# When a router is prepared, which engine copies sums, one projection at full height: four edits to a planned linear attention and mixture-of-experts kernel

## The chip, the cores and the metric

The kernel runs on one core of one Trainium2 chip. The core has a matrix engine (TensorE, PE in the profile; its weight loads, PEld, overlap the matmuls), a vector engine (VectorE, DVE), a scalar engine with activation functions (ScalarE, ACT), a general one (GpSimd, POOL), and SyncE (SP), which here only issues DMA transfers. Each engine runs its own instructions strictly in order; semaphores hold an instruction back until what it needs is there. The metric is the device time of one execution in microseconds (us), as the median of several runs. Before the change it is 818.04 us (817.71 to 819.43 in 3 runs).

## The reference

Three stages follow each other on 2304 tokens (4 batches of 576) of width 512 (8 heads of 64). Cut to what is computed:

```python
def phi(x):                                   # features, 64 -> 128
    proj = einsum('bhsd,md->bhsm', x, omega)
    h = proj - sum(x * x) / 2
    return exp(h - max(h)) / sqrt(m)
q_p, k_p = phi(q * scale), phi(k * scale)
kv = einsum('bhsm,bhsd->bhmd', k_p, v)        # sums over a batch's tokens
z = sum(k_p, axis=2)
x = einsum('bhsm,bhmd->bhsd', q_p, kv) / (einsum('bhsm,bhm->bhs', q_p, z) + 1e-6)

xn = x / sqrt(mean(x * x) + 1e-6) * rms_g     # a gated MLP, 512 -> 1536 -> 512
g = xn @ w_gate
x = (g * sigmoid(g) * (xn @ w_val)) @ w_out

logits = x @ w_gate2 + modality_bias[modality_id]   # top-1 of 8 experts, 512 -> 1024 -> 512
e = argmax(logits)
out = max(softmax(logits)) * (relu(x @ w1[e]) @ w2[e])
```

All inputs are float32 but the modality (int64); the output is float32.

## The kernel before, in words

**Tiles.** The tokens are 18 tiles of 128 (tiles 0 to 17). The attention takes k tiles and q tiles by name: k0 to k17, q0 to q17. Each tile has 8 heads in two units g = 0 and 1 of four heads. The order of the first nine is written out: "k0 k1 k2 k3 k4 q0 q1 q2 q3"; the others are woven into the MLP behind.

**One tile of the attention.** Its load (L520) brings x transposed, two heads (2 x 64 rows) on the 128 partitions. A projection (`projections`) multiplies it by omega in 8 products of 128 columns. omega is held twice in one tile of 128 x 256, as a block-diagonal matrix (`omega2`: rows 0 to 63 hold it in columns 0 to 127, rows 64 to 127 in columns 128 to 255, the rest is zero). So a projection can run in two forms: at full height (128 rows, L564, where the other head's rows meet zeros), which before is used for k0 and k1 alone, or at half height (64 rows, L571), used for all others. The trace counts two records for each product, sixteen for a tile. Then VectorE takes a maximum per head (L588), ScalarE the exponentials (L594). A k tile then adds its products with v to the batch's sums (L643, one group of eight records for each unit), a q tile is transposed (L609), copied out of the bank (L321 by `copy_on`), multiplied with the sums (L795) and divided (L820 and on).

**Seeds.** A batch has 576 tokens, so every other boundary falls in the middle of a tile. For a k tile that straddles two batches, the second batch's share is summed in a bank of its own and copied to a tile `seed` (L766, on VectorE); it is added when the batch's sums are closed.

**The router's small inputs.** `fetch_small` loads the router's weights, the modalities and the two biases. `bias_of_tokens` (L473 to L484) makes a bias for each token on VectorE, `split_route` (L486 to L490) splits the weights into three bfloat16 parts in five VectorE instructions (L489 and the subtraction in the helper `rest`, L325). Their first reader is the routing of the first finished tile (product L1328, scores L1348 to L1353), far later. The gain vector `rms_g` is loaded by `fetch_g` (L1403) and scaled on VectorE (L1409 to L1421).

**The MLP and the experts.** The MLP runs over 9 chunks of 256 tokens: transposes of its input (L1170), hidden products (L1192) for 12 blocks of 128 features, output products (L1262). All weights come as float32 and are split into two float16 halves (scalings and remainders on VectorE, ScalarE and GpSimd; L325 is the remainder's line on every engine). The tokens are then dealt to slots of 128 rows, one expert each: a first table for the tokens of tiles 0 to 15 (six "early" slots) and a full table later, whose place numbers end in the products of L1913. Each slot gathers its rows from memory by an indirect DMA on GpSimd (`gather`), is transposed, multiplied by the expert's matrices (up L2136, down L2165) and scattered to the output (L2033).

**What sets the order: a planner.** The kernel doesn't issue instructions in the order of its loops. Each step is an operation `plan.op(engine, cost, want, function, ...)` with a cost in us, a due number `want` and the buffers it reads and writes. `Plan.schedule` (L172 and on) plays the program through: whenever an engine is free it takes, of the operations whose inputs are ready and whose buffers can be had, the one with the smallest `want`. Where an operation may run on several engines (a dict of costs, engine `None`), whichever is free first takes it, but VectorE, in the main part, only when it has nothing of its own to do (`key`). An operation's users become ready `lag` after its end. The result is one fixed order per engine. Before that, `NUDGES` shifts due numbers: (first, last, shift, kind) adds `shift` to the operations of these numbers, of one kind if one is given.

**Padding.** `spare` plans 140 matmuls (L505) that nobody reads, with a due number of 1e9: the planner puts one wherever TensorE would otherwise have nothing ready. They stand in the program and always run.

**Loads.** SyncE issues the loads in one queue, in planned order. Eight semaphores are dealt to the transfers in turn, so a load may wait for an earlier one, and for TensorE or others who still read its buffer.

## Time and profile before

| | us |
|---|---|
| median of 3 runs (lowest, highest) | 818.04 (817.71, 819.43) |
| the profiled execution | 813.95 |
| its span | 812.2 |
| busy: TensorE | 795.9 |
| busy: VectorE | 546.5 |
| busy: ScalarE | 467.7 |
| busy: GpSimd | 290.3 |

The profile records one execution. The span runs from its first to its last instruction; the time of the execution has a little more around it. A timeline lists an engine's instructions as runs of one line: where it starts, how long it takes, and in brackets how long the engine was idle before it and what ended that. On TensorE neighbouring records overlap in their modelled ends, so the price of a group is read from its start to the start of the next. The list of waits adds up an engine's idle time by the instruction that waited and the one it waited for. A line of the page is that of the instruction, which for helpers is the helper's.

### The profile page before, as it was taken

Reading aid. Unit: us, or ns where it says so; the run is one execution under the profiler, and the core shown is the slowest. Engines: PE = TensorE matmul, PEld = TensorE weight load, DVE = VectorE, ACT = ScalarE, POOL = GpSimd, SP = SyncE. Lnnn points to the kernel's source line nnn. Section 1 sums busy time; section 2 is a strip of 40 time slices with the busy share of each in tenths; the row PEclk is TensorE's granted clock in tenths of the full one; section 3 lists DMA queues with packets and bytes.
Section 4 is the critical chain, followed back from the end, with each engine's and each line's share of the span. In section 5 each row is a group of like instructions: output and inputs, shape, how many; then the busy total and the mean of one; then the engine's idle time right before and its main releaser. Section 6 shows DMA issues by size and latency. Waiting matters only on the chain.

```text
span 812.2 us, 20349 instructions
## 1 busy us (share of the span) xinstructions
PE 795.9 (98%) x8128; PEld 627.9 (77%) x8128; DVE 546.5 (67%) x1299; ACT 467.7 (58%) x1118; POOL 290.3 (36%) x424
## 2 busy tenths in 40 slices
PE   9999999999999999999999999999999999999995
PEld 8999888988566878887878877777776778777772
DVE  5778888998348788898998888778767212222121
ACT  5767667777444777777787878666242322323221
POOL 0267898673213233223333343323222211212011
PEclk9999999999999999999999999999999999999998
DMA  8526341347111764776777677864726989999950
GB/s 279 173 62 234 136 143 40 96 157 287 47 40 54 250 218 130 246 273 223 234 229 235 201 240 230 272 245 181 280 75 266 411 295 406 425 410 425 425 228 29
DMA packets 37253, 179.31 MB, mean 221 GB/s; under 512 B 4863, under 2 KB 4991, under 8 KB 21280
## 3 DMA queue, kind: packets, MB, share of 16 engines
q1 hardware_dynamic: 34144, 168.33, 58.0%
q0 software_dynamic: 3008, 9.61, 3.2%
q8 instruction: 66, 1.08, 0.5%
q14 instruction: 35, 0.29, 0.1%
HBM read 134.90 MB, written 43.16 MB: 219 GB/s over the span
## 4 chain that ended last, share of the span: by engine, by line
PE 79%; DVE 6%; issue 5%; POOL 4%; DMA 4%; ACT 1%; POOLq 0%; ACTq 0%
PE bank L1192 28%; PE bank L1262 17%; PE bank L2136 8%; PE bank L2165 7%; PE bank L643 4%; PE bank L571 4%; DMA out_dram<-plain,x 2%; PE bank L795 2%; PE bank L505 2%; PE bank L609 2%; POOL plain L1230 1%; POOL big L325 1%; PE bank L1301 1%; PE bank L1995 1%; PE bank L1170 1%
## 5 line engine op out<-in xcount | busy, mean ns | idle before, releaser
L1192 PE MATMUL bank<-x,big 128*128 128x256 f16 x2592 | 307.3, 273 | 0.1
L1192 PEld LDWEIGHTS <-big 128*128 128x128 f16 x2592 | 250.2, 98 | 43.0 <-issue 0.7
L1262 PE MATMUL bank<-big 128*128 128x512 f16 x648 | 157.2, 379 | 0.0
L325 POOL TENSOR_TENSOR big<-plain,big 128x256 f16<-128x256 f32 x97 | 80.0, 827 | 135.1 <-ACT big L315 98.3
L880 DVE SCALAR_TENSOR_TENSOR big<-big,e_fac 128x512 f16<-128x512 f32 x128 | 102.6, 805 | 8.0 <-ACT big L886 6.5
L1262 PEld LDWEIGHTS <-big 128*128 128x128 f16 x648 | 62.4, 99 | 53.1
L2136 PEld LDWEIGHTS <-big 128*128 128x128 f16 x1632 | 95.6, 98 | 8.5
L2136 PE MATMUL bank<-plain,big 128*128 128x128 f16 x1632 | 100.6, 219 | 0.0
L2165 PE MATMUL bank<-big,plain 128*128 128x512 f16 x408 | 96.7, 379 | 0.0
L1211 ACT ACTIVATE plain<-bank,w_scale 128x256 f32<-128x256 f32 x108 | 50.6, 472 | 57.4 <-PE bank L1192 44.6
L1101 ACT ACTIVATE plain<-big,plain 128x1024 bf16<-128x1024 f32 x64 | 73.4, 1147 | 12.5 <-DMA big<-in_w_exp_dram 11.3
L325 DVE TENSOR_TENSOR plain<-plain 128x512 f16<-128x512 f32 (+2 forms) x42 | 27.3, 652 | 67.6 <-ACT plain L315 55.5
L594 ACT ACTIVATE plain<-bank,plain 128x128 f32<-128x128 f32 x216 | 61.1, 383 | 12.3 <-DVE plain L588 12.1
L886 ACT ACTIVATE big<-big,e_fac 128x512 f16<-128x512 f32 x95 | 67.8, 719 | 0.6 <-DMA split_dram<-big 0.6
L2165 PEld LDWEIGHTS <-plain 128*128 128x128 f16 x408 | 37.5, 98 | 35.7
L1216 DVE SCALAR_TENSOR_TENSOR plain<-plain,bank 128x256 f32<-128x256 f32 x108 | 44.4, 415 | 18.9 <-ACT plain L1211 13.7
L588 DVE TENSOR_REDUCE plain<-bank 128x4 f32<-128x512 f32 x72 | 47.8, 683 | 9.1 <-PE bank L564 4.8
L2153 ACT ACTIVATE plain<-bank 128x512 f32<-128x512 f32 x34 | 20.4, 599 | 57.0 <-PE bank L2136 55.1
L315 ACT CAST big<-plain 128x256 f16<-128x256 f32 x84 | 33.8, 405 | 29.6 <-DVE plain L1238 16.8
L325 DVE TENSOR_TENSOR plain<-bank,plain 128x512 f32<-128x512 f32 (+2 forms) x38 | 25.2, 666 | 29.6 <-ACT plain L315 29.3
L1230 POOL TENSOR_TENSOR plain<-plain,big 128x256 f32<-128x256 f32 x35 | 36.0, 1035 | 10.7 <-DVE plain L1216 9.7
L325 POOL TENSOR_TENSOR plain<-plain 128x512 bf16<-128x512 f32 (+1 forms) x22 | 24.7, 1124 | 32.4 <-DVE plain L325 22.7
(302 smaller groups left out, 1161.5 us busy)
## 6 DMA issues: line engine op xcount, KB each, us to landing
big<-split_dram SPq DMA_DIRECT2D x60, 1024.0 KB, 13.2
big<-in_w_exp_dram SPq DMA_DIRECT2D x32, 1024.0 KB, 6.5
split_dram<-big SPq DMA_DIRECT2D x32, 1024.0 KB, 8.6
big<-in_w_moe_dram SPq DMA_DIRECT2D x36, 512.0 KB, 3.7
x_dram<-plain SPq DMA_DIRECT2D x18, 258.0 KB, 3.1
plain<-in_qT_dram SPq DMA_DIRECT2D x14, 256.0 KB, 3.8
plain<-in_v_dram SPq DMA_DIRECT2D x13, 260.0 KB, 3.4
plain<-in_kT_dram SPq DMA_DIRECT2D x13, 256.0 KB, 4.3
```

The lines of the kernel that those rows point to most:

```text
L325: eng.tensor_tensor(out=out, in0=src, in1=hi, op=ALU.subtract)
L588: lambda: nc.vector.tensor_reduce(out=mx.tile, in_=pp.tile, axis=AX.X, op=ALU.min),
L594: nc.scalar.activation(ph[:, h, :], pp[:, h, :], AF.Exp, bias=mx[:, h : h + 1], scale=-1.0)
L880: nc.vector.scalar_tensor_tensor(out=out, in0=src, scalar=factor, in1=hi, op0=ALU.mult, op1=ALU.subtract)
L886: nc.scalar.activation(out, src, AF.Copy, scale=factor)
L1101: lambda c=c, h=h, cs=cs: nc.scalar.activation(junk.tile, raws[c][:, cs], AF.Square, bias=tiny, accum_out=sums[:, 2 * c + h : 2 * c + h + ...
L1192: nc.tensor.matmul(gv[:, t, :], w[a][:, kk, :], self.x[x][:, kk, :], start=kk == 0 and m == 0, stop=kk == KD - 1 and m == 2,)
L1211: lambda: nc.scalar.activation(th.tile, gv[:, 0, :], AF.Tanh, scale=one(BACK)),
L1216: lambda: nc.vector.scalar_tensor_tensor(out=th.tile, in0=th.tile, scalar=1.0, in1=gv[:, 0, :], op0=ALU.add, op1=ALU.mult,),
L1262: nc.tensor.matmul(self.acc[j].tile, h[:, a, r], out_w[f][:, i, :], start=f == 0 and m == 0, stop=f == FT - 1 and m == 2,)
L2136: nc.tensor.matmul(ph[:, j, :], w_of(c, p, k * F2 + (4 * n + j) * P, P), x[a][:, kk, :], start=kk == 0 and j == 0 and m == 0, stop=kk == K ...
L2165: nc.tensor.matmul(y.tile, hs[n][a][:, kk, :], w_of(2 + n, p, kk * DM, DM), start=f == 0 and m == 0, stop=f == KF2 - 1 and m == 2,)
```

## The change

Six edits. `WHOLE` becomes a list of names, "k0 k1 q1": the projection of q1 is done at full height as well. The due numbers of `bias_of_tokens` and `split_route` go from -150 and -140 to 28 and 29. The copies of the seeds may run on ScalarE or VectorE. The planner's lag of an early gather goes from 3 to 7. A pair of buffers (`qkx`) that nobody uses is gone. And `NUDGES` has 41 entries in place of 34, most with other numbers. The lines behind the table stand one line later in the changed kernel: L564 is L565.

```diff
--- before.py
+++ after.py
@@ -40,7 +40,7 @@
 THIRD_FROM, THIRD = 21.0, 0.65
 LAST_FROM, LAST = 26.5, 0.3
 EXACT = 6
-WHOLE = 2
+WHOLE = "k0 k1 q1"
 SPARE = 140
 NEARLY = 6
 NFULL = 17
@@ -50,15 +50,16 @@
 
 
 NUDGES = (
-    (927, 2712, 6.75, 61), (245, 713, 6.5, 39), (708, 753, 12), (252, 358, -9), (0, 1691, 7, 7),
...
+    (927, 2712, 6.75, 61), (247, 713, 6.25, 39), (250, 357, -8.25), (0, 1691, 7.5, 7),
...
 )
 
 
@@ -363,7 +364,7 @@
     STAGE, EXPERT = 36 * KB, 32 * KB
     area(
         "big", ("rawy", 8192, 2), ("bitsy", 4096, 2),
-        ("qkx", 2048, 2), ("phx", 2048, 2), ("ftx", 2048, 1),
+        ("phx", 2048, 2), ("ftx", 2048, 1),
         ("mxx", 16, 2), ("mod_i", 144, 1), ("mod_f", 208, 1), ("part", 576, 1),
         ("w_r", 128, 1),
     )
@@ -492,8 +493,8 @@
 
     plan.op("dma", 0.3, -170, fetch_small, writes=[mod_i, mod_f, w_r])
     route_b = Buf()
-    plan.op("dve", 0.5, -140, split_route, writes=[w_r, route_b])
-    plan.op("dve", 1.5, -150, bias_of_tokens, reads=[mod_i], writes=[mod_f, part, small_b])
+    plan.op("dve", 0.5, 29, split_route, writes=[w_r, route_b])
+    plan.op("dve", 1.5, 28, bias_of_tokens, reads=[mod_i], writes=[mod_f, part, small_b])
 
 
     def spare(n, before):
@@ -555,7 +556,7 @@
                 buf(named("ph", "phx"), [P, 4, NF], F32),
             ))
 
-        whole = kind == "k" and i < WHOLE
+        whole = f"{kind}{i}" in WHOLE.split()
 
         def products():
             for j in range(NPAIR):
@@ -762,9 +763,9 @@
                 acc = buf("acc", [P, 4, D + 1], F32)
                 kv_add(b, straddle[gg], whole[1][0], gg, *whole[1][1:], True, True, want, acc)
                 plan.op(
-                    "dve", 0.35, want,
-                    lambda acc=acc, gg=gg: nc.vector.tensor_copy(
-                        seed[:, 4 * gg : 4 * gg + 4, :], acc.tile
+                    {"act": 0.33, "dve": 0.35}, None, want,
+                    lambda e, acc=acc, gg=gg: copy_on(
+                        e, seed[:, 4 * gg : 4 * gg + 4, :], acc.tile
                     ),
                     reads=[acc], fills=[seed],
                 )
@@ -2009,7 +2010,7 @@
                     in_offset=bass.IndirectOffsetOnAxis(ap=ix[:rows, 0, col : col + 1], axis=0),
                 ),
                 reads=[ix, *(x2_b[:TE] if early else x2_b)], writes=[xg],
-                lag=3.0 if early else 8.0,
+                lag=7.0 if early else 8.0,
             )
             return xg
 
```

SyncE's queue of the start, before the change, with what each transfer waits for (big is the area that holds the tiles loaded first, DMAHW an earlier transfer's semaphore, PE the progress of TensorE):

```order
L528 DMA big_103<-in_v_dram 128x520 [waits DMAHW2_49]
L520 DMA big_103<-in_kT_dram 128x512 [waits DMAHW4_49,DMAHW3_49,PE_49]
L520 DMA big_103<-in_qT_dram 128x512
L520 DMA big_103<-in_qT_dram 128x512 [waits DMAHW5_49,PE_49]
L528 DMA big_103<-in_v_dram 128x520 [waits DMAHW6_49,PE_49]
L520 DMA big_103<-in_qT_dram 128x512 [waits DMAHW7_49]
L520 DMA big_103<-in_qT_dram 128x512 [waits DMAHW0_49,PE_49]
L1403 DMA plain_97<-in_rms_g_dram 128x512 [waits DMAHW1_49]
L528 DMA big_103<-in_v_dram 128x520 [waits DMAHW2_49,PE_49]
L542 DMA big_103<-in_v_dram 64x520 [waits DMAHW3_49]
L542 DMA big_103<-in_v_dram 64x520 [waits DMAHW4_49]
```

And after it:

```order
L529 DMA big_103<-in_v_dram 128x520 [waits DMAHW2_49]
L521 DMA big_103<-in_kT_dram 128x512 [waits DMAHW3_49,PE_49]
L521 DMA big_103<-in_qT_dram 128x512 [waits DMAHW5_49,DMAHW4_49,PE_49]
L529 DMA big_103<-in_v_dram 128x520 [waits DMAHW6_49,PE_49]
L521 DMA big_103<-in_qT_dram 128x512 [waits DMAHW7_49,PE_49]
L521 DMA big_103<-in_qT_dram 128x512
L521 DMA big_103<-in_qT_dram 128x512 [waits DMAHW0_49]
L529 DMA big_103<-in_v_dram 128x520 [waits DMAHW1_49]
L543 DMA big_103<-in_v_dram 64x520 [waits DMAHW2_49]
L543 DMA big_103<-in_v_dram 64x520 [waits DMAHW3_49,PE_49]
L1404 DMA plain_97<-in_rms_g_dram 128x512 [waits DMAHW4_49]
```

The last of the whole v tiles (128x520) stands ahead of the gain vector now, and waits for an earlier transfer alone; before, it stood behind the gain vector and waited for TensorE too. The second k tile, further up in the queue, now goes out ahead of the first weights.

VectorE near 25 us, before the change, from the end of `bias_of_tokens` on (plain holds the attention's working tiles, route_w the split weights, the banks are TensorE's results):

```order
L484 TENSOR_TENSOR bias_tok_70<-bias_tok_70,big_103 128x144
L766 COPY plain_97<-bank4_93 128x260
L489 CAST route_w_69<-big_103 128x4x8
L325 TENSOR_TENSOR big_103<-big_103,route_w_69 128x32
...
L489 CAST route_w_69<-big_103 128x4x8
L588 TENSOR_REDUCE plain_97<-bank0_89 128x4
L588 TENSOR_REDUCE plain_97<-bank1_90 128x4
L766 COPY plain_97<-bank4_93 128x260
L321 COPY plain_97<-bank6_95 128x512
L588 TENSOR_REDUCE plain_97<-bank5_94 128x4
```

And after it:

```order
L485 TENSOR_TENSOR bias_tok_70<-bias_tok_70,big_103 128x144
L589 TENSOR_REDUCE plain_97<-bank2_91 128x4
L589 TENSOR_REDUCE plain_97<-bank1_90 128x4
L490 CAST route_w_69<-big_103 128x4x8
L326 TENSOR_TENSOR big_103<-big_103,route_w_69 128x32
...
L490 CAST route_w_69<-big_103 128x4x8
L322 COPY plain_97<-bank4_93 128x260
L322 COPY plain_97<-bank6_95 128x512
L589 TENSOR_REDUCE plain_97<-bank0_89 128x4
L821 TENSOR_SCALAR plain_97<-bank6_95 128x4
```

The weights' split stays behind the bias, but the reductions of a query tile's projection (L589) have moved ahead of it, and one of the two copies of 260 columns is gone from VectorE; the other stands behind the split.

VectorE near 604 us, before the change, from the routing of a late tile to the start of the full table (xs and x01 hold the tables, logits and lmax the router's result):

```order
L1559 TENSOR_TENSOR xs_161<-logits_71,lmax_72 128x16
L1563 TENSOR_TENSOR xs_161<-xs_161 128x16
L1566 TENSOR_REDUCE xs_161<-xs_161 128x2
L1570 TENSOR_TENSOR xs_161<-xs_161 128x16
L325 TENSOR_TENSOR plain_97<-plain_97 128x512
...
L1365 TENSOR_SCALAR plain_97<-plain_97 128x512
...
L1370 MEMSET plain_97 128x3
L1765 COPY x01_576<-bank4_93 128x8
L1766 TENSOR_TENSOR x01_576<-x01_576,xs_161 128x1
```

And after it:

```order
L1560 TENSOR_TENSOR xs_134<-logits_71,lmax_72 128x16
L1564 TENSOR_TENSOR xs_134<-xs_134 128x16
L1567 TENSOR_REDUCE xs_134<-xs_134 128x2
L1571 TENSOR_TENSOR xs_134<-xs_134 128x16
L326 TENSOR_TENSOR plain_97<-plain_97 128x512
L326 TENSOR_TENSOR plain_97<-bank0_89,plain_97 128x512
...
L1366 TENSOR_SCALAR plain_97<-plain_97 128x512
...
L1371 MEMSET plain_97 128x3
L1766 COPY x01_571<-bank4_93 128x8
L1767 TENSOR_TENSOR x01_571<-x01_571,xs_134 128x1
```

Between the routing and the table's first copy there stands one more remainder of 512 columns, out of bank 0.

## Rows read from the trace of the kernel before

**Rows 1.** The page, busy time of each engine, its share of the span, instructions:
```profile
PE 795.9 (98%) x8128; PEld 627.9 (77%) x8128; DVE 546.5 (67%) x1299; ACT 467.7 (58%) x1118; POOL 290.3 (36%) x424
```

**Rows 2.** TensorE's waits; columns: total us, number of waits, longest us:
```profile
PE bank L1913 <- DVE x L1900: 1.7, 1, 1.7
...
PE bank L795 <- ACT plain L315: 0.9, 1, 0.9
PE bank L609 <- ACT plain L594: 0.7, 1, 0.7
PE bank L643 <- DMA big<-in_v_dram: 0.5, 1, 0.5
...
PE bank L1170 <- DVE plain L854: 0.2, 1, 0.2
```

**Rows 3.** TensorE's timeline, 0:62; columns: start us, length us, instruction [idle before <-releaser]:
```profile
7.40 2.10 PE L505 MATMUL bank<-ones_w,ones_h 128*128 128x252 bf16 x18
9.33 1.95 PE L564 MATMUL bank<-om,big 128*128 128x128 f32 x16
11.12 1.00 PE L643 MATMUL bank<-big,plain 128*128 128x65 f32 x8
...
22.49 1.11 PE L643 MATMUL bank<-big 128*128 128x65 f32 x8 [0.54 <-DMA big<-in_v_dram]
...
24.32 2.84 PE L643 MATMUL bank<-big,xs 128*128 128x65 f32 x24
27.10 1.16 PE L571 MATMUL bank<-om,big 64*128 64x128 f32 x16
28.19 1.11 PE L643 MATMUL bank<-big,xs 128*128 128x65 f32 x8
```

**Rows 4.** The timeline of TensorE and GpSimd, 800:813:
```profile
801.93 0.49 PE L505 MATMUL bank<-ones_w,ones_h 128*128 128x252 bf16 x3
...
803.14 0.98 POOL L2033 DMA_INDIRECT out_dram<-plain,x  x1 [4.58 <-ACTq L2205]
```

**Rows 5.** The timeline of SyncE's queue, 8:21:
```profile
16.26 0.42 SPq L1403 DMA_DIRECT2D plain<-in_rms_g_dram  x1
17.65 0.33 SPq L528 DMA_DIRECT2D big<-in_v_dram  x1
```

**Rows 6.** The chain that ended last, in order of time:
```profile
17.65 4.79 DMA big<-in_v_dram
```

**Rows 7.** VectorE's timeline, 21:31:
```profile
21.36 0.68 DVE L1409 TENSOR_REDUCE g_near<-plain 128x1 f32<-128x512 f32 x1
...
23.11 1.28 DVE L588 TENSOR_REDUCE plain<-bank 128x4 f32<-128x512 f32 x2
24.30 0.17 DVE L475 CAST big<-big 128x18 f32<-128x18 int32 x1
...
27.27 0.43 DVE L766 COPY plain<-bank 128x260 f32<-128x260 f32 x1 [1.36 <-PE bank L643]
27.62 0.17 DVE L489 CAST route_w<-big 128x32 bf16<-128x32 f32 x1
...
28.59 1.28 DVE L588 TENSOR_REDUCE plain<-bank 128x4 f32<-128x512 f32 x2
```

**Rows 8.** TensorE's timeline, 168:172:
```profile
170.37 0.66 PE L1170 MATMUL bank<-ident,plain 128*128 128x128 f32 x4 [0.17 <-DVE plain L854]
```

**Rows 9.** TensorE's timeline, 600:640:
```profile
603.04 1.46 PE L2165 MATMUL bank<-big,plain 128*128 128x512 f16 x6
604.33 1.50 PE L2136 MATMUL bank<-plain,big 128*128 128x128 f16 x24
...
622.55 0.25 PE L1913 MATMUL bank<-x,xs 128*128 128x62 bf16 x3 [1.70 <-DVE x L1900]
```

**Rows 10.** VectorE's timeline, 602:624:
```profile
605.02 0.69 DVE L325 TENSOR_TENSOR plain<-plain 128x512 f16<-128x512 f32 x1 [0.26 <-ACT plain L315]
...
621.76 0.73 DVE L1900 TENSOR_TENSOR x<-x,xs 128x558 bf16<-128x558 bf16 x1
```

17 rows, old and new, of the table NUDGES are left out of this document.

## The prediction

> **What bounds the kernel now.** I read the page's busy shares first. TensorE is busy for 98% of an 812.2 us span, and no other engine reaches 70% [rows 1]. So a gain needs either fewer instructions on TensorE or fewer moments in which it stands still. Next I read the list of what TensorE waited for. It has nine rows, which add up to 6.4 us in all; the largest is one wait of 1.7 us for VectorE (DVE) late in the program [rows 2]. The rest of the time can only go if TensorE's own stream gets shorter. Third, I read the timeline of TensorE's first 60 us, because there the stream holds padding: the matmuls of L505, which nobody reads. 131 of the 140 stand in the first 62 us and 9 at the program's end. They run whether or not TensorE would have had to wait, so in the early part the time of a later matmul is the sum of what stands ahead of it plus the waits. Between 24 and 86 us there is no wait at all. The sum is therefore a count.
>
> The profiled execution took 813.95 us; the median of the three runs is 818.04, 4.09 us above it. I work in differences against the profiled execution and add them to the median.
>
> **The change part by part.** All prices are starts to starts.
>
> *Padding.* In the new order 126 padding matmuls stand in the early part and 14 at the end: 5 have moved, chiefly out of the group between the first two projections (18 before, 8 now directly behind both). A group of 18 starts at 7.40 and the next instruction at 9.33, so one costs 0.107 us [rows 3]: -0.54. The five come back behind the last useful matmul. The three that stand there now begin at 801.93 and the last scatter is issued at 803.14 [rows 4]; five more take until about 802.8, and the scatter waits for ScalarE (ACT), not for them. Without that cover they would give the 0.54 back.
>
> *The second query tile at full height.* Sixteen L571 records (64 rows) take from 27.10 to 28.19, 1.09; sixteen L564 records (128 rows) take from 9.33 to 11.12, 1.79, at the same clock [rows 3]: +0.70. Nothing hides it, since TensorE doesn't wait there. Ahead of the L571 group the row shows something more: the 24 matmuls of L643 take 2.78 us, 0.116 each, against 0.112 for the L564 records, so some 0.1 us stands before the switch of height. The Trainium skill, TensorEngine Tiling (Array Packing), section Key Properties, says that changing the tiling mode drains the engine; a tile at full height between full-height neighbours would save that drain, and the term would be +0.6. The trace shows a gap of that size, and not whether the drain makes it. By the rule the whole sum would be 0.1 lower.
>
> *Loads at the start.* The second k tile is now loaded ahead of the first weights, and the fourth v tile ahead of the gain vector. That v tile is the one load that TensorE waited for: 0.54 us at 22.49 [rows 2, 3]. It was issued at 17.65, after waiting for TensorE, and landed 4.79 us later [rows 5, 6]. In the new queue it waits for an earlier load alone. Adding up TensorE's new stream (k0 to 7.40, k1 1.79, 8 padding 0.86, k2 1.09, four products and three padding 2.2, k3 1.09) gives 14.4 for the end of k3's projection. The q load behind that, two more and the v load follow at about 0.45 apart: issue near 15.8, landing near 20.6. TensorE reaches the product at 14.4 + 0.86 + four groups of products of 0.94 + two projections of 1.09, which is 21.2. The wait goes: -0.54. If the landing took three microseconds more than before, it would be +1.7.
>
> *Router's bias and weights.* Their due numbers change from before everything to 28 and 29, but the order of DVE shows them at the same place: DVE had nothing else ready there, and the planner filled the hole. They take 1.6 us from 24.30 and 1.0 from 27.62 [rows 7]. What is new is what stands behind them. The gain vector's load is issued behind the v loads, near 18.8 instead of 16.26 [rows 5]. With v's 4.79 to landing it comes at 23.6; its six DVE instructions (21.36 to 23.11 before, 1.75) end at 25.4 and the bias at 27.0. Then come the two reductions of the second query tile (1.28), the weights (1.0), a copy of sums (0.4) and the copy of the first query tile's transposes (0.7): 30.4. TensorE has finished that query tile near 26.7, and then has two groups of products, four transposes and a projection ahead of the product that needs the copy, 3.5: 30.2. I take +0.25, near the middle: 0 if the gain vector lands as early as before, +1.4 if weights and copy are paid in full.
>
> *Copies of the sums.* Three of four copies of 0.43 go to ACT. The first two stand in an idle stretch of DVE of 1.36 [rows 7], the others at 246 us, where TensorE does not wait. Nothing; 0.4 either way if one meets a tile that TensorE needs.
>
> *From 40 to 127 us* DVE, GpSimd and ACT run in the old order but for two pairs on ACT, and TensorE but for one pair. The waits of 0.9 and 0.7 us for ACT (L795, L609) lie there [rows 2]. Everything shifts together, so they stay.
>
> *From 127 us on* the new nudges deal the order anew, and 148 operations change engine: 67 go from DVE to ACT and 56 back. One wait is at a place that I can name: the transposes of L1170 at 170.37, idle 0.17 for DVE [rows 8]. They now stand 13 us of matmuls later: -0.17. The large one, 1.70 at L1913 [rows 9], looks as if it should go, since the table now stands some 6 us of TensorE work later. It does not, because its whole chain moves with it. From the remainder at 605.02 to the end of the last operand at 622.49 DVE stands still nowhere [rows 10]. The new order puts one more such remainder of 0.69 us into that chain (0.6 net of overlap). On TensorE the stretch from the last routing product to the table gains a group of four transposes, about 0.5, and has three groups of L2136 (1.50) in place of three of L2165 (1.46), 0.1 [rows 9]. Both sides grow by 0.6: 0, with -0.6 and +0.6 as the ends if one of them is wrong.
>
> *Gathers planned longer* changes only where the planner puts what reads them. None of the nine rows of waits names a gather: 0. At most one gets a wait of the size of those for ACT, +0.9.
>
> Sum: -0.54 + 0.70 - 0.54 + 0.25 - 0.17 = -0.30. From 818.04 that is 817.7 us.
>
> **The rivals.** *The later stretch sheds its waits (faster).* The early part gains the same, and the L1913 wait of 1.70 goes as well: 816.0. For it: that is the largest single wait, and the order around it is quite different. Against it: the chain begins with the routing, which moved too, and got longer. It decides from 1.3 us of those 1.7 on.
>
> *ACT becomes the one that is waited for (slower).* Eleven more operations come to ACT from DVE than go the other way, most of them scalings of the experts' weights between 265 and 560 us, where they queue ahead of the exponentials and tanhs whose results free TensorE's banks. Price: each operation of TensorE that meets such a queue waits 0.7 to 0.9, the two such rows (L609, L795) [rows 2]. Three of them make +2.4: 820.1. For it: ACT works in strict order and these two waits came at a place where it was not its own bound. Against it: ACT is busy for 58% of the span [rows 1], and TensorE has several groups between most producers and their readers. It decides from three such waits on; two give 819.3.
>
> *The edit of the router does not do what it says.* The order shows that already, and it is in the sum as such.
>
> **How the numbers follow.** A measurement of this kernel can tell some 0.2%, 1.6 us, from no change, so no change reaches from 816.4 to 819.7. The forecast has 0.50; a faster outcome 0.30 (the waits from 127 us on shed, or more than one of the terms at its low end: no row fixes the new order of that stretch, so this is not small); a slower one 0.20 (ACT, or the v load and the gain vector both late: +1.7 + 0.54 and +1.15 on the sum, 821.1). The likeliest case's own range is 816.4 to 819.7. To leave out no more than 2 in 10 it reaches into both others: below to 814.4, where the waits at L1913, L795 and L609 are all gone (-1.7 - 0.9 - 0.7), above to 820.9, just short of both loads late.
>
> **What would show it.** In the new profile: 126 padding matmuls before 62 us and 14 at the end; a group of sixteen L565 records of 1.79 us near 25 us; no wait of TensorE for a v load; a small wait or none at the first L796; the waits at L610, L796, L957 as before and about 0.1 us earlier; none at L1171; the wait at L1914 still 1.5 to 2 us; ACT's busy time up and DVE's down by some 5 to 15 us. I am wrong if the L1914 wait is gone, if waits for ACT add up to more than 4 us, or if the first hidden product (L1193) starts over 1 us from its old place.

## The result and the profile after

The changed kernel takes 821.95 us (median of 7 runs, 820.59 to 822.92) against 818.54 for the kernel before, measured beside it: a ratio of 1.0051, interval 1.0037 to 1.0065. It is slower by half a per cent, clear of the noise, and above the range of the prediction. One thing belongs to the result from the start: repeated on chip 1 the ratio is 1.0057 and 1.0052, repeated on chip 4 it is 1.0006 (0.9989 to 1.0023). The first result doesn't name its chip.

The profiled execution took 822.59 us, 8.64 more than that of before, with a span of 820.8. Section 1 of its page answers to [rows 1]:

```profile
PE 801.0 (98%) x8128; PEld 631.9 (77%) x8128; DVE 545.5 (66%) x1289; ACT 471.0 (57%) x1129; POOL 290.4 (35%) x423
```

TensorE has the same 8128 matmuls and is 5.1 us longer busy with them. The list of its waits in the kernel after answers to [rows 2] (total us, number, longest):

```profile
PE bank L796 <- ACT plain L316: 1.5, 2, 1.0
PE bank L2062 <- ACT plain L2154: 1.5, 2, 0.7
PE bank L1914 <- DVE x L1901: 1.4, 1, 1.4
PE bank L506 <- DVE plain L448: 1.3, 1, 1.3
PE bank L2166 <- ACT plain L887: 1.1, 1, 1.1
PE bank L2091 <- issue: 1.1, 3, 0.4
PE bank L1193 <- DVE plain L628: 0.7, 1, 0.7
PE bank L610 <- ACT plain L595: 0.6, 1, 0.6
```

Four rows are new: L2062, L2166, L2091 and L1193. "issue" is a pause for which the profile shows no releaser. The v load's row is gone, and so are those of L957 (0.5 before) and L1171. The rows that name ACT add up to 4.7 us, where they made 2.1 before (L795, L609, L956).

Some lines of the experts' part, for what follows: L2154 is the relu behind a slot's up products, L2166 its down products, L887 the scaling of a finished slot, L2034 its scatter, L2007 a gather, L316 a cast. L2062 and L2091 are the up and down products of the slots of 64 rows, the half slots. (In the kernel before, each stands one line earlier, in runs that add code a few lines later.)

**The first 62 us.** TensorE's timeline of the kernel after, beside [rows 3]:

```profile
9.22 1.02 PE L506 MATMUL bank<-ones_w,ones_h 128*128 128x252 bf16 x8
...
18.67 2.00 PE L644 MATMUL bank<-big 128*128 128x65 f32 x16
20.60 1.16 PE L572 MATMUL bank<-om,big 64*128 64x128 f32 x16
...
23.53 1.95 PE L644 MATMUL bank<-big,xs 128*128 128x65 f32 x16
25.32 2.00 PE L565 MATMUL bank<-om,big 128*128 128x128 f32 x16
27.16 1.90 PE L644 MATMUL bank<-big,xs 128*128 128x65 f32 x16
...
54.15 1.04 PE L1193 MATMUL bank<-x,big 128*128 128x256 f16 x8
```

The group between the first projections has 8 padding matmuls for 18. The second query tile at full height takes 25.32 to 27.16, 1.84 against a forecast of 1.79. The first hidden product starts at 54.15, where it was 54.42 before.

**The table.** TensorE, VectorE (DVE) and ScalarE (ACT) in the kernel after, the place of [rows 9]:

```profile
628.89 1.46 PE L2166 MATMUL bank<-big,plain 128*128 128x512 f16 x6
630.98 0.73 DVE L1901 TENSOR_TENSOR x<-x,xs 128x558 bf16<-128x558 bf16 x1
631.63 0.68 DVE L326 TENSOR_TENSOR plain<-plain 128x512 f16<-128x512 f32 x1
631.77 0.25 PE L1914 MATMUL bank<-x,xs 128*128 128x62 bf16 x3 [1.42 <-DVE x L1901]
632.35 0.60 ACT L2154 ACTIVATE plain<-bank 128x512 f32<-128x512 f32 x1 [2.73 <-DVE plain L326]
632.84 0.68 ACT L887 ACTIVATE plain<-bank,plain 128x512 f32<-128x512 f32 x1
633.58 1.46 PE L2166 MATMUL bank<-big,plain 128*128 128x512 f16 x6 [1.10 <-ACT plain L887]
```

Where one wait of 1.70 stood, there are two, 2.52 together, 0.82 more. TensorE's second wait is for a scaling (L887) whose data were ready; it stood in ACT's queue behind a relu (L2154) that waited 2.73 for VectorE. The relu reads only a bank of TensorE; what held it is the remainder L326, which by the kernel's code reads the buffer that the relu writes. That remainder stood in VectorE's queue behind the chain to the table (its last operand is L1901) and ran from 631.63 on.

**The pauses.** TensorE, GpSimd (POOL) and ACT in the kernel after:

```profile
683.16 1.46 PE L2166 MATMUL bank<-big,plain 128*128 128x512 f16 x6
683.22 0.97 POOL L2007 DMA_INDIRECT plain<-x_dram,x  x1 [0.31 <-issue]
684.02 0.58 ACT L316 CAST plain<-bank 128x512 f16<-128x512 f32 x1 [3.83 <-PE bank L2137]
685.35 1.56 PE L2062 MATMUL bank<-plain,big 128*128 128x64 f16 x48 [0.73 <-ACT plain L2154]
...
694.33 1.01 POOL L2034 DMA_INDIRECT out_dram<-plain,x  x1 [0.47 <-PE bank L2091]
695.21 1.51 PE L2091 MATMUL bank<-plain,big 128*128 128x64 f16 x37
695.64 0.97 POOL L2007 DMA_INDIRECT plain<-x_dram,x  x1 [0.30 <-issue]
697.15 0.48 PE L2091 MATMUL bank<-plain,big 128*128 128x64 f16 x11 [0.43 <-issue]
697.47 1.23 PE L2137 MATMUL bank<-plain,big 128*128 128x128 f16 x19
```

The 48 matmuls of a group of L2091 take from 695.21 to 697.47, 2.26 us, and stop once in the middle. The six of L2166 from 683.16 take 2.19 to the next instruction, where six others take 1.29. Each time a gather (L2007) starts 0.3 us behind the end of another indirect DMA. The same two places come again at 724 and 736: four losses of 0.86 to 0.94, 3.6 us. At L2062 TensorE waits for a relu, and that relu is late because what ACT gets from TensorE is late: the cast ahead of it starts 0.86 us behind the end of the products that it was waiting for (683.16, the start of the next group); in the profile of after_third, shown below, it is 0.14. Behind 640 us there are 8 such close pairs, and four have no pause.

**The clock.** Two profiles of the same changed kernel, the one of the result and then after_again, by stretches (us; TensorE, weight loads, DVE, ACT, POOL; the granted clock; DMA share; GB/s):

```profile
244.00:246.00 2.00, 2.00 (x19) 2.00 (x19) 0.96 (x4) 0.38 (x1) 1.10 (x2) 0.50 0.03 8
```
```profile
244.00:246.00 2.00, 2.00 (x35) 1.88 (x35) 1.82 (x9) 0.74 (x2) 0.38 (x2) 1.00 0.08 23
```

In the first the clock stands at its lower level (0.50, 1.2 GHz), in the second at 2.4. The stretch from the 13 matmuls of L644 there to the next L695 takes 7.60 us in the one and 4.49 in the other. So 3.1 of the 8.64 us are this execution's, not the change's: a later profile of the kernel before (before_again) falls to 0.50 at the same place too. Another 1.0 lies behind the last scatter's issue (810.82 against 803.14, a difference of 7.68); from there to the end of the span profiles of either kernel take 8.5 to 10.0. The 7.68 are then -0.3 to the first hidden product, about +0.3 between 115 and 180 us, +3.1 clock, +0.8 at the table and +3.6 pauses: 7.5.

The clock has a second such place, which the profile of the result doesn't show. It is the table: TensorE's timeline in after_fourth, and one stretch of it with the columns as above:

```profile
632.30 2.49 PE L2166 MATMUL bank<-big,plain 128*128 128x512 f16 x6 [1.11 <-ACT plain L887]
634.58 2.18 PE L2137 MATMUL bank<-plain,big 128*128 128x128 f16 x24
636.60 1.46 PE L2166 MATMUL bank<-big,plain 128*128 128x512 f16 x6
...
633.00:634.00 1.00, 1.00 (x4) 0.33 (x3) 0.97 (x4) 0.00 (x0) 0.90 (x1) 0.50 1.02 418
```

Behind the two waits (1.41 and 1.11) the clock stands at 0.50, and the two groups take 4.30 us from start to start of the next, where they take 2.63 in the profile of the result (633.58 to 636.21). Nine of the profiles in this document have both waits at the table. Four of them show this (after_fourth, y2_third, y2_again, z3_scatter_spaced, at 1.65 to 1.67 us each, on chips 1, 4 and 7), and none of the other eleven does, which have no wait for L887. So the second wait costs more in some executions than its own length.

### The profile page after: what moved, and what is told of

It is laid out like the page before. It is cut to its first block, busy times and chain, and to the rows that moved or that the text cites. A ratio compares the mean times of both kernels' runs of the same rounds, so it can differ in the third digit from the quotient of the medians.

```text
span 820.8 us, 20353 instructions
## 1 busy us (share of the span) xinstructions
PE 801.0 (98%) x8128; PEld 631.9 (77%) x8128; DVE 545.5 (66%) x1289; ACT 471.0 (57%) x1129; POOL 290.4 (35%) x423
## 4 chain that ended last, share of the span: by engine, by line
PE 72%; issue 10%; DVE 7%; POOL 5%; DMA 3%; ACT 1%; SPq 0%; POOLq 0%; DVEq 0%
PE bank L1193 27%; PE bank L1263 17%; PE bank L2137 5%; PE bank L2166 5%; PE bank L644 4%; PE bank L572 4%; DMA out_dram<-plain,x 2%; PE bank L796 2%; PE bank L506 2%; PE bank L610 2%; POOL plain L1231 2%; POOL big L326 1%; PE bank L1302 1%; DMA big<-in_v_dram 1%; PE bank L1171 1%
## 5 line engine op out<-in xcount | busy, mean ns | idle before, releaser
L1193 PE MATMUL bank<-x,big 128*128 128x256 f16 x2592 | 304.9, 273 | 0.7 <-DVE plain L628 0.7
L1193 PEld LDWEIGHTS <-big 128*128 128x128 f16 x2592 | 250.1, 98 | 39.2 <-issue 1.6
L1263 PE MATMUL bank<-big 128*128 128x512 f16 x648 | 153.6, 379 | 0.0
L326 POOL TENSOR_TENSOR big<-plain,big 128x256 f16<-128x256 f32 x99 | 80.0, 812 | 147.4 <-ACT big L316 115.5
L2166 PE MATMUL bank<-big,plain 128*128 128x512 f16 x408 | 98.5, 379 | 1.1 <-ACT plain L887 1.1
L887 ACT ACTIVATE big<-big,e_fac 128x512 f16<-128x512 f32 x97 | 68.5, 721 | 0.1
L595 ACT ACTIVATE plain<-bank,plain 128x128 f32<-128x128 f32 x196 | 54.8, 377 | 16.9 <-DVE plain L589 16.9
L2166 PEld LDWEIGHTS <-plain 128*128 128x128 f16 x408 | 37.6, 98 | 34.6 <-issue 1.2
L326 DVE TENSOR_TENSOR plain<-bank,plain 128x512 f32<-128x512 f32 (+2 forms) x38 | 25.3, 667 | 51.5 <-ACT plain L316 40.3
L2154 ACT ACTIVATE plain<-bank 128x512 f32<-128x512 f32 x34 | 20.3, 598 | 65.0 <-PE bank L2137 56.9
L316 ACT CAST big<-plain 128x256 f16<-128x256 f32 x88 | 35.1, 405 | 38.5 <-DVE plain L1239 15.7
L589 DVE TENSOR_REDUCE plain<-bank 128x4 f32<-128x512 f32 x71 | 46.9, 683 | 13.9 <-PE bank L572 8.7
L326 DVE TENSOR_TENSOR plain<-plain 128x512 f16<-128x512 f32 (+2 forms) x43 | 28.1, 655 | 39.3 <-ACT plain L316 39.1
L316 ACT CAST plain<-bank 128x512 f16<-128x512 f32 (+2 forms) x33 | 18.6, 563 | 47.7 <-PE bank L2137 27.5
L891 DVE TENSOR_SCALAR plain<-bank,plain 128x512 f32<-128x512 f32 (+1 forms) x13 | 9.7, 749 | 52.7 <-PE bank L2166 36.3
```

The lines of the kernel that those rows point to most:

```text
L316: nc.scalar.mul(out, src, factor) if factor != 1.0 else nc.scalar.copy(out, src)
L326: eng.tensor_tensor(out=out, in0=src, in1=hi, op=ALU.subtract)
L589: lambda: nc.vector.tensor_reduce(out=mx.tile, in_=pp.tile, axis=AX.X, op=ALU.min),
L595: nc.scalar.activation(ph[:, h, :], pp[:, h, :], AF.Exp, bias=mx[:, h : h + 1], scale=-1.0)
L887: nc.scalar.activation(out, src, AF.Copy, scale=factor)
L1193: nc.tensor.matmul(gv[:, t, :], w[a][:, kk, :], self.x[x][:, kk, :], start=kk == 0 and m == 0, stop=kk == KD - 1 and m == 2,)
```

## The experiments

Theory A: ACT's order makes the new waits (the rival of the prediction). Theory B: the order behind 590 us, which one entry of the table of nudges sets, brings indirect DMAs close together, and TensorE pauses there. Theory C: what pauses depends on the chip as well. The first four runs number their own theories: 1 is the experts' slots, 2 the fall of the clock near 243 us, 3 the edits of the first 60 us. "The five edits" are those beside the table of nudges.

**One entry exchanged** (chip 1, before 817.47). x1_late_old is the changed kernel with an entry of the old table in place of one of the new; x2_late_new is the kernel before with the reverse. The two repeats ran beside them.

```diff
-    (881, 898, 6.25), (707, 741, 16), (2583, 3207, -19.75, 106), (179, 1488, -12, 35),
+    (881, 898, 6.25), (707, 741, 16), (2658, 3207, 15.25, 109), (179, 1488, -12, 35),
```

> The changed kernel with one entry of the nudges put back: (2658, 3207, 15.25, 109), which delays the experts' up products, in place of (2583, 3207, -19.75, 106), which brings the transposes of the gathered rows forward. Up to about 590 us the order of every engine is that of the changed kernel, behind it that of the kernel before. Theory 1 (the loss sits in the experts' slots): the waits of TensorE at the half slots (0.73, 0.43, 0.73, 0.19, 0.43 us and what goes with them, 3.6 us in all) and the wait of 1.10 at L2166 go; the time falls by 4 to 5 us from the changed kernel's, to 817 to 818, about 0.5 to 1 under the kernel before. Theory 2 (the loss is the fall of TensorE's clock near 242 us, 2.8 us in the changed kernel's profile): the order there is unchanged, so the fall stays and the time stays within 1.5 us of the changed kernel, 820.5 to 822. Theory 3 (the edits of the first 60 us cost it: q1 at full height, the router's inputs later): also 820.5 to 822, with the loss visible by 62 us.

> The mirror: the kernel before with that one entry of the new nudges, so its order up to about 590 us and the changed kernel's order behind it. Theory 1: the half slots wait as in the changed kernel, and the time is 4 to 5 us above the kernel before, 822 to 823.5. Theories 2 and 3: the time stays within 1.5 us of the kernel before.

> The kernel before once more, unchanged, for what one profile can show by chance. Time 0.998 to 1.002 of the kernel before. Theory 1: TensorE waits at no half slot in this profile either. Theory 2, if the fall of the clock belongs to the new order: no fall between 200 and 300 us here; if it is a matter of chance of one execution, a fall may show here as well, costing about 3 us.

> The changed kernel once more, unchanged. Time 1.004 to 1.007 of the kernel before. Theory 1: the waits at the half slots come again at the same instructions, with 3 to 4 us in all. Theory 2: the clock falls again at about 242 us; if it does not and the time is the same, that fall is not what makes the difference.

Measured: x1 817.90, ratio 1.0006 (0.9985 to 1.0026); x2 820.94, 1.0038 (1.0018 to 1.0059); before_again 818.34, 1.0005 (0.9983 to 1.0027); after_again 822.20, 1.0057 (1.0038 to 1.0076). The loss goes with the entry in both directions: exchanging it takes away 4.3 us (822.20 to 817.90), and brings 3.5 to the old kernel (817.47 to 820.94, less than the 822 that was expected at least). x1 keeps all five edits and the new order up to 590 us, so these together cost nothing that can be measured, and theory 3 is out. The profile of after_again has no fall of the clock, and its execution takes 821.27 us all the same, so theory 2 is out. The waits of x2 at the half slots repeat those of the changed kernel, though all ahead of 590 us is the old order:

```profile
PE bank L2061 <- ACT plain L2153: 1.8, 2, 1.2
...
PE bank L2090 <- issue: 1.0, 3, 0.5
```

The second wait at the table did not come with the entry: x2 has one wait of 1.91 there. That wait needs the entry (x1 hasn't got it) and the rest of the new order too.

**ACT's order, and the distance of the DMAs** (chip 7, before 815.79). y1_relu_first moves two casts behind the relus that L2062 waits for. y2_spaced puts two additions on GpSimd (1.33 us for both) ahead of each later gather; y3_late_old_spaced does the same in x1, y4_before_spaced in the kernel before.

```diff
...
+            for cast, relu in ((2943, 2904), (3041, 3002)):
+                o = next(o for o in done if o.n == cast)
+                done.remove(o)
+                done.insert(next(i for i, x in enumerate(done) if x.n == relu) + 1, o)
...
```
```diff
...
+            def fetch():
+                if not early and plan.nudged:
+                    for _ in range(2):
+                        nc.gpsimd.tensor_tensor(
+                            out=rest_tile, in0=rest_tile, in1=rest_tile, op=ALU.add
+                        )
...
```

> The changed kernel, with two operations of ScalarE moved: at the first two half slots the cast of the next slot's rows is issued behind the relu of the slot before and not ahead of it. Nothing else moves. Theory A (ScalarE's strict order makes the loss at the half slots): the waits of TensorE at the half slots' up products (L2062; 0.53 to 0.73 us each) go, and the time falls by 1 to 1.8 us. Theory B (TensorE and its signals stand still for 0.6 to 0.9 us whenever GpSimd issues a gather right behind another indirect DMA, 0.3 us after its end): the waits at L2062 shrink, since a cast of 0.58 us has left the chain behind the late signal, but the stalls in the down products (L2091, two idle times of about 0.15 and 0.43 at 695 to 697 and at 737 to 739 us) stay as they are; the time falls by at most 1.2 us.

> The changed kernel, with two additions of 128x256 on GpSimd (about 1.0 us each, on a tile that nobody reads) ahead of each gather of the slots behind the early ones. The orders of TensorE, VectorE and ScalarE stay as they are; only the pair of scatter and gather is pulled apart from 0.3 to some 2.4 us. Theory A: the waits at L2062 stay at 0.5 to 0.7, the time stays within 0.2% of the changed kernel. Theory B: the stalls in L2091 are gone and the waits at L2062 fall to 0.3 or less, so TensorE needs 2.5 to 3.5 us less behind 640 us; the time is 818.5 to 820. If the gathers come too late by the delay, new waits of the transposes L1996 for the gathered rows would show.

> The changed kernel with the old entry of the nudges for the experts (run x1_late_old) and the same two additions ahead of each later gather. Theory B: the excess of TensorE behind 630 us that was left in that run (0.65, 0.67 and 0.91 us, each with a gather 1.3 us behind another indirect DMA) goes, and the time falls by about 1.5 to 2 us from that run's, to 816 to 816.5, which would be 0.1 to 0.2% under the kernel before. Theory A: no change from that run, 817.9.

> The kernel before with the same two additions ahead of each later gather. Theory B: the stalls that its second profile showed (0.68 at 659 us and 0.92 at 715 us, each with a gather 1.3 us behind another indirect DMA) go, and none appears elsewhere behind 630 us; the time falls by up to 1.5 us, to 816 to 817.5, and the spread of its runs gets narrower. Theory A: unchanged, 0.999 to 1.001.

Measured: y1 818.07, 1.0023 (1.0000 to 1.0046); y2 817.91, 1.0022 (1.0007 to 1.0038); y3 816.50, 1.0004 (0.9985 to 1.0022); y4 815.54, 0.9998 (0.9981 to 1.0015). No profile of the four has a pause, y1's neither, whose DMAs are as close as before. So these runs can't tell A from B: chip 7 seemed to have no pauses to take away, though the changed kernel itself was not run on it. That was the first sign of C. The additions themselves cost nothing that can be measured (y4).

**The table's wait, the old table, and scatters spaced** (chip 7, before 815.65). z1_three_moves is y1 and moves the scaling L887 ahead of the relu that it stood behind. z2_old_nudges has the five edits with the whole old table of nudges. z3_scatter_spaced puts the additions ahead of the first 15 scatters, so ACT's order and the close gathers stay.

```diff
...
+            o = next(o for o in done if o.n == 2778)
+            done.remove(o)
+            done.insert(next(i for i, x in enumerate(done) if x.n == 2807), o)
...
```
```diff
-    (927, 2712, 6.75, 61), (247, 713, 6.25, 39), (250, 357, -8.25), (0, 1691, 7.5, 7),
+    (927, 2712, 6.75, 61), (245, 713, 6.5, 39), (708, 753, 12), (252, 358, -9), (0, 1691, 7, 7),
...
```
```diff
...
+            def put():
+                if many < 15 and plan.nudged:
+                    for _ in range(2):
+                        nc.gpsimd.tensor_tensor(
+                            out=rest_tile, in0=rest_tile, in1=rest_tile, op=ALU.add
+                        )
...
```

> The changed kernel with the two moves of the run y1_relu_first, and a third on ScalarE: at the full table, near 632 us, the scaling of a finished slot (L887) is issued ahead of the relu that waits for VectorE (L2154), and not behind it. Theory A (ScalarE's strict order makes the loss behind 600 us): the wait of 1.1 us at L2166 goes as well, and the time is 1.1 us under that of y1_relu_first, at a ratio of about 1.001 to the kernel before; the half slots show neither waits nor stalls, as in y1_relu_first. Theory B (a gather 0.3 us behind another indirect DMA makes TensorE stand still): the wait at L2166 goes too, but some of the five pairs of scatter and gather near 660, 682, 694, 722 and 734 us show a stall of 0.4 to 0.9 us again, since their distance is unchanged.

> The changed kernel with the whole old table of nudges, so the other five edits alone (q1 at full height, router's inputs due later, seeds' copies on either engine, the lag of 7, the unused area gone). The order is dealt anew, but at the half slots it is that of the kernel before. If the nudges make the loss (theories A and B alike), the half slots show no waits at L2062, the table no wait at L2166, and the time is within 0.2% of the kernel before, 816 to 819 if that runs at 817.5. If the five edits make it (theory 3), it is slower by 0.3 to 0.6%.

> A control of y2_spaced: the same two additions on GpSimd, now ahead of each scatter of the first 15 slots in place of ahead of each gather. The work added and the delay of the gathers are about the same, but scatter and gather stay 0.3 us apart. Theory B: the stalls in L2091 and the waits at L2062 are there as in the changed kernel, at least three of the four, and the time is that of the changed kernel, ratio 1.004 to 1.007. If they are gone here too, it isn't the distance of the pair that makes them, and theory B falls: then any shift in time of these transfers is enough.

Measured: z1 816.39, 1.0003 (0.9985 to 1.0022); z2 818.84, 1.0039 (1.0017 to 1.0061); z3 817.79, 1.0027 (1.0011 to 1.0043). In z1 the second wait at the table is gone and the first is 1.36; from the start of the last routing product to the end of the last L2166 it takes 193.04 us against 194.30 in y1, 1.26 less. z1's line at the place of the second wait, which names no wait (the move puts it at L2175):

```profile
633.87 1.46 PE L2175 MATMUL bank<-big,plain 128*128 128x512 f16 x6
```

With that one move on ACT the ratio goes from 1.0023 to 1.0003, level with the old kernel, though the two intervals overlap. z3 keeps the cast ahead of the relu and L2062 doesn't wait: ACT's order alone doesn't make the waits at L2062 (on chip 1 it lengthens them, see z1_third). z3 was meant as the control of y2, and as such it tells nothing: without pauses on chip 7 there was nothing to keep or lose, and it was not run on chip 1. z2 missed its expectation (within 0.2%), which by its own words speaks for theory 3; x1 speaks against that, and z2 is slow by places of its own, as TensorE's timeline shows:

```profile
594.65 0.70 PE L505 MATMUL bank<-ones_w,ones_h 128*128 128x252 bf16 x5
596.40 0.65 PE L1995 MATMUL bank<-ident,plain 128*128 128x128 f32 x4 [1.04 <-DVE plain L867]
```

The nine padding matmuls that stood at the end have come to 594 us, directly ahead of a wait of 1.04 that they don't fill. A table of nudges fits one order only; with the five edits the old one lands elsewhere.

**Chip 4** (before 816.74): the changed kernel, y2, z1 and x1 again, unchanged.

> The changed kernel a third time, in one call with three of the kernels below, since the runs y1 to z3 were made without it at their side, and there TensorE paused at no pair of scatter and gather whatever the edit. Theory C (the pauses depend on the chip or the loading of a call, not on the edits): no pauses behind 640 us here either, and a ratio of 1.002 to 1.003 to the kernel before. Theory B or A (the edits took them away): the pauses at about 683, 696, 725 and 737 us are here again, and the ratio is 1.005 to 1.006.

> The changed kernel with the additions ahead of each later gather, again. Theory B: no pauses, 2 to 3 us under after_third of this call. Theory C: as after_third, within 0.15%, unless pauses show in after_third and not here.

> The changed kernel with the three moves on ScalarE, again; its pairs of scatter and gather stay 0.3 us apart. Theory B: if after_third shows pauses, this one does too at some pairs. Theory C: whether it shows them goes with after_third. In both the wait of 1.1 us at L2166 is gone, and the time is at least 1 us under after_third; under theory A 3 to 4 us.

> The changed kernel with the old entry of the nudges for the experts, again. The order theory holds if it is under after_third of this call by 1 us or more whatever the pauses do (the wait at L2166 is gone by the order). With pauses in after_third the difference should be 3 to 4 us as in the first call, without them 1 to 2.

Measured: after_third 817.86, 1.0006 (0.9989 to 1.0023); y2_again 817.30, 1.0012 (0.9995 to 1.0030); z1_again 816.00, 0.9997 (0.9976 to 1.0018); x1_again 816.13, 1.0002 (0.9982 to 1.0022). The intervals overlap throughout. What decides is the timeline of after_third at the places that were shown above:

```profile
681.36 1.46 PE L2166 MATMUL bank<-big,plain 128*128 128x512 f16 x6
681.50 0.58 ACT L316 CAST plain<-bank 128x512 f16<-128x512 f32 x1 [3.12 <-PE bank L2137]
...
691.63 1.01 POOL L2034 DMA_INDIRECT out_dram<-plain,x  x1 [0.47 <-PE bank L2091]
692.51 1.56 PE L2091 MATMUL bank<-plain,big 128*128 128x64 f16 x48
692.94 0.97 POOL L2007 DMA_INDIRECT plain<-x_dram,x  x1 [0.30 <-issue]
693.91 1.28 PE L2137 MATMUL bank<-plain,big 128*128 128x128 f16 x20
```

The same instructions, the gather again 0.30 behind the scatter, and the 48 matmuls take 1.40 without a stop. The close pair alone does nothing; the chip has to do with it. The second wait at the table stands in this profile too (1.11), and x1_again and z1_again, which haven't got it, are 1.7 and 1.9 us under after_third.

**Chip 1 again** (before 818.43): the changed kernel, y2 and z1, unchanged.

> The changed kernel a fourth time, on whatever chip this call gets. On a chip where TensorE pauses behind 640 us (as in the first profile and in after_again): ratio 1.005 to 1.006, pauses of 0.4 to 0.9 us near 683, 696, 725 and 737 us. On one where it does not (as in after_third): ratio 1.000 to 1.003, and only the wait of 1.1 us at L2166 in the experts' stretch.

> The changed kernel with the additions ahead of each later gather. If after_fourth of this call pauses: theory B says that this one does not and is 2.5 to 3.5 us faster; theory C (the chip alone decides) says that it pauses as well, and is as slow. If after_fourth does not pause, both are alike within 0.2%, and the two theories stay undecided.

> The changed kernel with the three moves on ScalarE, pairs of scatter and gather 0.3 us apart. If after_fourth pauses: this one pauses at the down products L2091 too under theories B and C (up to 2 us), and gains 1.1 us at L2166 and about 1.2 us at the two L2062; under theory A it shows none. If after_fourth does not pause: 1 to 2 us under it.

Measured: after_fourth 822.06, 1.0052 (1.0033 to 1.0070); y2_third 819.36, 1.0016 (1.0002 to 1.0030); z1_third 819.28, 1.0010 (0.9995 to 1.0025). The same place in y2_third:

```profile
694.50 1.01 POOL L2043 DMA_INDIRECT out_dram<-plain,x  x1 [0.47 <-issue]
695.39 1.56 PE L2100 MATMUL bank<-plain,big 128*128 128x64 f16 x48
695.53 1.33 POOL L2010 TENSOR_TENSOR rest_tile<-rest_tile 128x256 f32<-128x256 f32 x2
697.00 0.98 POOL L2013 DMA_INDIRECT plain<-x_dram,x  x1
```

and in z1_third, where the pair is close:

```profile
693.53 1.45 PE L2100 MATMUL bank<-plain,big 128*128 128x64 f16 x37
693.97 0.97 POOL L2016 DMA_INDIRECT plain<-x_dram,x  x1 [0.30 <-issue]
695.39 0.49 PE L2100 MATMUL bank<-plain,big 128*128 128x64 f16 x11 [0.41 <-issue]
```

With the pair pulled apart there is no pause on this chip either; where it is close, the group stops after its 37th matmul as before. z1_third keeps two pauses at L2100 (L2091 of the changed kernel) and has lost the two waits at L2062. TensorE's signal is late there as before (at 682 us the relu starts 0.81 behind the end of its products), but with the cast out of its way TensorE loses only 0.17 and 0.19, where after_fourth loses 0.87 and 0.63. So on chip 1 the additions ahead of the gathers are worth 2.7 us (822.06 to 819.36), and z1's three moves 2.8; the table's wait (1.26) and the two shortened losses (1.1) make 2.4 of that, and the fall of the clock at the table, which z1's profiles don't have, may be in the rest. What the additions change is the distance from scatter to gather and also the gather's moment; with z3 not run on chip 1, the two are not separated.

Which of the close pairs pause can be read in the profiles of chip 1 and of the result (seven, from 640 us on). Some scatters had to wait for an earlier one to land before GpSimd issued them. Of the 19 pairs that begin with such a scatter none costs TensorE anything; of the 29 others 26 do. The pair at 661 us shows both. Its scatter in the profile of the result and in after_again:

```profile
660.97 1.03 POOL L2034 DMA_INDIRECT out_dram<-plain,xs  x1 [1.29 <-DMA out_dram<-plain,xs]
```
```profile
659.60 1.03 POOL L2034 DMA_INDIRECT out_dram<-plain,xs  x1 [0.20 <-issue]
```

Behind the first nothing stops, behind the second TensorE loses 0.89. Why is not known.

No version is measurably faster than the kernel before: the lowest ratios are 0.9997 (z1_again) and 0.9998 (y4).

## Why the prediction was wrong

**The padding and the full-height tile** came nearly as worked out. The first hidden product is 0.27 earlier, by the four terms up to there it would be 0.13. One part of the difference is the gap ahead of a change of height: sixteen L644 take 1.93 ahead of the 64-row group at 20.60 and 1.79 ahead of the 128-row group at 25.32. That is the gap of 0.14 which the prediction left out of its sum. The Trainium skill, TensorEngine Tiling (Array Packing), section Key Properties, has a change of tiling mode drain the engine; by that rule the term is +0.6. The trace agrees in size (1.84 - 1.09 - 0.14 = 0.61), and does not show whether a drain makes the gap.

**The loads.** The v wait is gone in the profile of the result, and 0.2 to 0.5 in the three later profiles of the changed kernel, so -0.54 was the good end. The gain vector's reduction starts at 23.09 (forecast 23.6), the router's work ends in time, and the first L796 runs at 30.52 without a wait: the +0.25 was not paid. Both errors are within 0.5 us. The bad end of the v load's term comes out of its own figures as about +1.8, not +1.7 (20.6 + 3 - 21.2 - 0.5).

**The failed step is "From 127 us on".** It named one wait that would go (L1170; it went) and argued that the table's wait stays and nothing else comes. Three things came:
- Small waits in the new order, above all 0.68 at L1193 and 0.46 at L796. The waits of 115 to 180 us add up to 2.52 against 2.18.
- The wait at the table did stay (1.42 against 1.70), but TensorE's next instruction waits 1.10 for ACT. This is the mechanism of the slower rival, once, and not where that rival put it (265 to 560 us). It was to be read from the order: L887 stands there behind a relu that needs a remainder from the end of the late DVE chain. I followed that chain to the table and not to the others who wait for it. The term was 0 and measured +0.8 by the waits; the second wait by itself is 1.3 (z1 against y1), and 1.65 more in the executions in which the clock falls behind it.
- The pauses, 3.2 to 4.1 us in the profiles of the changed kernel that show them, against 1.6 (0.68 and 0.91) in before_again on chip 1.

**"None of the nine rows of waits names a gather: 0"** failed with it. The reasoning took the list of waits as all that a gather can cost. The pauses have no releaser, or are put down to the relu that ended last; the profile of before which I had shows none at all. What the order could have shown is that behind 640 us 8 gathers follow close on another indirect DMA, where 5 did before. I did not count them, and no row at hand would have given them a price. x1 shows that the longer plan for gathers by itself does nothing here: it is in x1, and the cost is not.

**The signs.** One of the signs of being wrong came: the waits for ACT add up to 4.7 us, over the 4 that were named, and to 3.2 in after_third, without the pauses. The wait at L957 went, where it was to stay; L1914 is just under its 1.5 to 2. On chip 4 the changed kernel's 817.86 lies inside the range and next to the 817.7. That would have been luck: the second wait at the table is there too, and that step is just as wrong.

**Busy times.** ACT rose by 3.3 us and DVE fell by 1.0, where I expected 5 to 15 for each: 67 operations went one way and 56 came back.

**Shown and not shown.** Shown: the loss lies behind 590 us, goes with one entry in the new order, and is made of the table's second wait (z1, chip 7) and, on chip 1, of the pauses, which go when the gathers are delayed (y2_third). An estimate for chip 1 from these rows: the start and 115 to 180 us cancel, the table gives 0.8, the pauses 1.6 to 2.5 more than in before_again, together 2.4 to 3.3, and 1.65 where the clock falls at the table; measured are 3.9 (822.20 against 818.34). Not shown: what in the chip stops TensorE, whether it is the distance of the two DMAs or the moment of the second, why a scatter that had to wait spares the pair, and why no pair pauses on chips 4 and 7. The first profile of the changed kernel fits chip 1, and that of the kernel before, without a pause at pairs where before_again has two, fits the others; neither names its chip.

## What to carry to other kernels

When a planner deals an order anew, follow each late producer to every queue that waits for it, not just to the one wait that the old profile names; on an engine in strict order a ready operation behind a waiting one is a new wait. A loss of half a per cent may belong to one chip: run both kernels again elsewhere before explaining it, and compare two profiles of the same kernel before reading a difference of two single ones. Indirect DMAs that GpSimd issues back to back may be worth pulling apart: on chip 1 it gained 2.7 us, and on the others it cost nothing that could be measured.

## What the runs showed of the hardware

- On chip 1 TensorE lost 0.6 to 1.0 us at four or five places of an execution of the changed kernel, each time where GpSimd issued a gather 0.30 us behind the end of another indirect DMA: idle in the middle of a group of matmuls with no releaser in the profile, or with its results reaching ACT about 0.7 us later than without the pause. With 2.5 us from start to start (y2_third) there was none. Pairs whose scatter had waited for an earlier one to land cost nothing (19 of 19). Chips 4 and 7 showed no pause.
- The granted clock fell to 0.50 near 243 us in some executions of either kernel and not in others, for up to 6.8 us, in a stretch in which TensorE ran narrow 64-row products (L644, 64x65) without standing still; it cost 3.1 us in the profile of the result.
- It fell to 0.50 at the table too, in four of nine profiles in which TensorE had just stood still for 1.4 and 1.1 us, and in none of the other eleven; each time it cost 1.65 to 1.67 us.
- The kernel before itself differs between chips: 815.7 on chip 7, 816.7 on chip 4, 817.5 to 818.4 on chip 1.
